# Issue-order edges and four dummy matmuls at the start of a transformer-block kernel

## Chip, cores, metric

The kernel runs on one core of a Trainium2 chip. The metric is the device time of one execution in microseconds (us); lower is better. The span that a profile shows, from the first to the last instruction, is about 1.8 us shorter than the device time of the same execution (739.5 against 741.27 us in the profile before).

Engines are named as in the profile: PE is TensorE's matmul, PEld its weight loads, DVE is VectorE, ACT is ScalarE, POOL is GpSimd, SP is SyncE.

## The reference

One block: layer norm, a projection to q, k and v, linear attention with 32 heads, an output projection with a residual, then layer norm, a gated feed-forward part and a second residual. Inputs are bf16; S = 2048 tokens, D = 1024, F = 3584.

```python
phi = lambda t: jnp.where(t > 0, t + 1, jnp.exp(t)) + 1e-6
q, k, v = split_heads(layernorm(x) @ wqkv)
kv  = einsum("bhsd,bhse->bhde", phi(k), v);  z = einsum("bhsd->bhd", phi(k))
h   = x + merge_heads((phi(q) @ kv) / (phi(q) . z + 1e-6)) @ wo
n   = layernorm(h)
out = h + (relu(n @ W_gate) * (n @ W_up)) @ W_down
```

## The kernel before

The change touches only the start of the kernel. There, tokens come in tiles of 128. A tile is normalised, transposed so that its features lie on the partitions, and multiplied with the K weights. The first four tiles are transposed on PE through one PSUM buffer, later ones by DMA. The first tile is normalised on VectorE, the others on ScalarE. Sixteen dummy matmuls on zeros run before the first data have come.

```python
    PE_T = 4          # tiles that PE transposes
    SPIN = 16         # dummy matmuls
    ...
        load_x(atiles[0])            # order of the loads
        load_w(wk_sb, 0, D)          # K weights, first column half
        load_x(atiles[1])
        load_w(wk_sb, 1, D)          # K weights, second column half
        load_x(atiles[2])
        load_x(atiles[3])
        for j in range(2):
            load_w(wv_sb, j, 2 * D)

        def ln_T(t):
            ...
            for k in range(2):       # VectorE: statistics of two halves, then their aggregate
                nc.vector.bn_stats(out=stats[:, k, :], in_=x_sb[:, k * NW:(k + 1) * NW])
            nc.vector.bn_aggr(out=mv[:], in_=stats[:])
            nc.scalar.activation(out=lnv, in_=mv[:, 1:2], func=ACT.Ln, bias=LN_EPS, scale=1.0)
            nc.scalar.activation(out=rstd, in_=lnv, func=ACT.Exp, scale=-0.5)
            if t == atiles[0]:
                ...                  # VectorE normalises tile 0 in two halves
                transpose_in(t, xn)
                return
            nc.vector.scalar_tensor_tensor(out=nmr, in0=mv[:, 0:1], scalar=-1.0, in1=rstd, op0=ALU.mult, op1=ALU.mult)
            nc.scalar.activation(out=xn[:], in_=x_sb[:], func=ACT.Identity, bias=nmr, scale=rstd)
            ...                      # later tiles: transposed by DMA
            transpose_in(t, xn)

        def transpose_in(t, xn):
            s, i, r = place(t)
            for k in range(2):       # one PSUM buffer ("D", bufs=1) for all halves
                pt = pspool.tile([P, KH, P], BF16, tag="D", bufs=1, name="tp")
                for kc in range(KH):
                    nc.tensor.transpose(pt[:, kc, :], xn[:, (k * KH + kc) * P:(k * KH + kc + 1) * P], ident[:])
                (nc.scalar.copy if k else nc.vector.tensor_copy)(
                    out=xT[s][i][:, k * KH:(k + 1) * KH, r:r + P], in_=pt[:])
    ...
        def k_plain(t):              # K of one tile: 8 matmuls for each column half
            ...
            for j in range(2):
                ps = pspool.tile([P, NW], FP32, tag="AE"[j], bufs=2, name="kp")
                for kc in range(KC):
                    nc.tensor.matmul(ps[:], lhsT=xT[s][i][:, kc, r:r + P], rhs=wk_sb[:, kc, js], ...)
                ...                  # exp on ScalarE, two VectorE instructions
    ...
        with tc.high_priority():
            ...
            for n in range(SPIN):
                nc.tensor.matmul(spin[:], lhsT=zero[:, 0:P], rhs=zero[:], start=True, stop=True)
            ln_T(atiles[0])
        ln_T(atiles[1])
        todo = atiles[2:8]
        for t in units[0]:
            k_plain(t)
            ln_T(todo.pop(0))
        new_v(0)
        for n, t in enumerate(units[0]):
            v_plain(t)
            ...
            if n == 1:
                sums_unit(1)
                k_sums()             # VectorE: sums of K weights, needed by the units after the first
```

The order in this text isn't the order on VectorE: the scheduler has brought the first of the four `k_sums` additions (L133 in the profile) forward, and it runs among the first tiles, at 10.77 us.

## Time and profile before

| What | Value | Where it is read |
|---|---|---|
| time, three executions | 740.27 us median (739.84 to 740.81) | the timed runs |
| time of the profiled execution | 741.27 us, mean clock 0.998 | the profile's own run |
| PE busy | 724.0 of 739.5 us (98%) | page, part 1 |
| longest PE wait after the dummies began, in the first 45 us | 2.1 us, for the copy of tile 0's first half | list of waits |
| granted clock, 9.58 to 13.14 us | 0.52 | table of stretches |

How to read PE busy: the records of pipelined matmuls overlap in it. K matmuls that start 0.22 us apart are listed with 0.38 us each. So it doesn't measure the distance from PE's peak. Here it serves only to find stretches in which PE has nothing to do, and for these it is good enough.

The timeline of PE in the kernel before, at its start. The columns are start, length, engine, line, operation, tiles, shapes, count, and in brackets the idle time before it and what ended it.

```profile
5.42 1.83 PE L400 MATMUL spin<-zero 128*128 128x512 bf16 x6
7.09 0.39 PE L299 MATMUL tp<-ident,xn 128*128 128x128 bf16 x4
9.58 0.58 PE L299 MATMUL tp<-ident,xn 128*128 128x128 bf16 x4 [2.10 <-DVE xT L300]
9.96 3.18 PE L347 MATMUL kp<-pq_mem,xT 128*128 128x512 bf16 x7
12.94 0.41 PE L299 MATMUL tp<-ident,xn 128*128 128x128 bf16 x4
13.20 0.38 PE L347 MATMUL kp<-pq_mem,xT 128*128 128x512 bf16 x1
```

Tile 0's first four transposes end at 7.48 us, the second four can't start before the buffer is copied out, and PE stands still for 2.1 us. Then seven K matmuls take 3.18 us, about 0.43 us from one start to the next, twice the 0.22 us of the warm ones later on. A column half of K needs one half of the weights.

The timeline of VectorE over the same time shows why the copy was late.

```profile
7.71 1.29 DVE L272 BATCH_NORM_STATS2 stats<-x_sb 128x6 f32<-128x512 bf16 x2 [1.24 <-DMA x_sb<-in_A_x_dram]
9.03 0.21 DVE L274 BATCH_NORM_AGGREGATE mv<-stats 128x2 f32<-128x12 f32 x1
9.16 0.37 DVE L300 COPY xT<-tp 128x512 bf16<-128x512 bf16 x1
...
10.77 1.23 DVE L133 TENSOR_TENSOR pq_mem<-pq_mem 128x2048 f16<-128x2048 bf16 x1 [0.87 <-DMA pq_mem<-in_A_wqkv_dram]
13.40 0.42 DVE L300 COPY xT<-tp 128x512 bf16<-128x512 bf16 x1 [1.40 <-PE tp L299]
```

The copy at 9.16 stands in VectorE's queue behind tile 1's statistics, although VectorE was idle for 1.24 us before these. L133 waits for the second half of the K weights, so its start, 10.77, marks when that half has landed.

The table of stretches of the kernel before. After the stretch and its length come the busy time of PE with the number of instructions, the same for PEld, DVE, ACT and POOL, then the granted clock, the DMA share and GB/s.

```profile
7.10:9.58 2.48, 0.38 (x6) 0.26 (x4) 1.78 (x4) 0.28 (x2) 0.00 (x0) 1.00 1.09 351
9.58:13.14 3.56, 3.56 (x15) 1.64 (x14) 1.38 (x2) 1.84 (x3) 0.00 (x0) 0.52 1.07 361
13.14:20.00 6.86, 6.66 (x42) 3.22 (x41) 6.60 (x17) 4.56 (x11) 0.00 (x0) 1.00 1.08 365
```

The clock of 0.52 in the second row is the half speed that the K matmuls showed.

### The profile page before, as it was taken

What the parts mean: (1) busy time and instruction counts of PE and PEld (TensorE: products, weight loads), DVE (VectorE), ACT (ScalarE), POOL (GpSimd) and SP (SyncE); (2) the same over time, 40 slices, a digit from 0 to 9 for tenths busy, and PEclk for the clock granted to TensorE, in tenths of its full rate; (3) what the DMA queues carried; (4) which work ended last, traced back from release to release, by engine and by line L of the source; (5) the groups of instructions that cost most, each with busy time, mean ns of one, the idle gap of its engine ahead of it and who ended that gap; (6) DMA issues with size and microseconds to landing.
All of it is one profiled execution on the core that took longest, in us unless ns stands there. A gap on an engine that the chain in (4) does not pass through costs nothing.

```text
span 739.5 us, 10552 instructions
## 1 busy us (share of the span) xinstructions
PE 724.0 (98%) x3967; PEld 382.7 (52%) x4020; DVE 563.7 (76%) x992; ACT 321.5 (43%) x580; POOL 5.6 (1%) x44
## 2 busy tenths in 40 slices
PE   8999999999999999999999999999999999999997
PEld 3444555444444444444444444444444458888566
DVE  5997644676798767778778777877786479996797
ACT  4877554778887644434344444444445120000000
POOL 0000000000000000000000000000000000000000
PEclk9999999999999999999999999999999999999999
DMA  9666002169987426164638359575583399987822
GB/s 315 153 145 170 1 1 67 48 149 218 237 168 181 124 73 206 43 193 134 198 117 242 110 177 283 171 219 194 170 277 121 129 398 339 331 288 299 295 76 82
DMA packets 146594, 132.02 MB, mean 179 GB/s; under 512 B 50928, under 2 KB 128112, under 8 KB 146544
## 3 DMA queue, kind: packets, MB, share of 16 engines
q1 hardware_dynamic: 135536, 123.30, 55.4%
q10 hardware_dynamic: 11008, 8.06, 3.4%
q8 instruction: 31, 0.51, 0.3%
q14 instruction: 19, 0.16, 0.1%
HBM read 79.95 MB, written 39.85 MB: 162 GB/s over the span
## 4 chain that ended last, share of the span: by engine, by line
PE 78%; DVE 8%; ACT 7%; DMA 5%; issue 1%; SPq 0%; DVEq 0%; POOL 0%; ACTq 0%
PE accA L821 22%; PE accY L821 8%; PE accX L821 8%; PE accA L1153 8%; PE Aq L314 3%; PE accA L982 3%; PE attn L557 3%; PE accX L1153 3%; PE Aq L454 3%; PE accY L1153 2%; DMA hn<-hn 2%; ACT hn L570 2%; PE Eq L314 2%; PE accY L982 2%; PE accX L982 2%
## 5 line engine op out<-in xcount | busy, mean ns | idle before, releaser
L831 ACT ACTIVATE gu<-gu 128x512 bf16<-128x512 bf16 x72 | 45.4, 631 | 131.4 <-DVE gu L830 131.4
L826 ACT COPY snap<-accA 128x1024 f32<-128x1024 f32 x72 | 72.5, 1008 | 36.4 <-PE accA L821 36.3
L821 PEld LDWEIGHTS <-tu 128*128 128x128 f16 x384 | 37.6, 98 | 45.3
L821 PEld LDWEIGHTS <-tg 128*128 128x128 f16 x384 | 37.6, 98 | 45.3
L557 PE MATMUL attn<-wo_mem,oT 128*128 128x512 bf16 x247 | 58.1, 379 | 2.3 <-DVE o_sb L534 1.0
L830 DVE TENSOR_TENSOR gu<-accY,snap 128x1024 bf16<-128x1024 f32 x36 | 43.9, 1220 | 10.0 <-ACT snap L826 10.0
L821 PE MATMUL accA<-hn,tu 128*128 128x512 f16 (+1 forms) x192 | 49.3, 379 | 0.0
L821 PE MATMUL accA<-hn,tg 128*128 128x512 f16 (+1 forms) x192 | 49.3, 379 | 0.0
L830 DVE TENSOR_TENSOR gu<-accX,snap 128x1024 bf16<-128x1024 f32 x36 | 43.9, 1219 | 6.3 <-PE accX L821 3.7
L154 ACT COPY u<-Aq 128x512 f32<-128x512 f32 x54 | 31.1, 580 | 36.2 <-PE Aq L314 19.3
L1153 PEld LDWEIGHTS <-x 128*128 128x128 f16 (+1 forms) x448 | 43.8, 98 | 5.5
L821 PEld LDWEIGHTS <-wg 128*128 128x128 bf16 x288 | 28.2, 98 | 34.0
L821 PEld LDWEIGHTS <-wu 128*128 128x128 bf16 x288 | 28.2, 98 | 34.0
L557 PEld LDWEIGHTS <-oT 128*128 128x128 bf16 x256 | 24.6, 97 | 32.2 <-issue 4.1
L834 DVE TENSOR_TENSOR hq<-gu 128x512 bf16<-128x512 bf16 x48 | 20.3, 423 | 14.3 <-ACT gu L831 14.2
L314 PEld LDWEIGHTS <-xT 128*128 128x128 bf16 (+1 forms) x192 | 18.6, 98 | 23.8 <-issue 2.4
L534 DVE TENSOR_TENSOR o_sb<-nd,rd 128x384 bf16<-128x384 f32 (+1 forms) x48 | 23.2, 509 | 8.6 <-ACT rd L533 6.6
L1153 PEld LDWEIGHTS <-xs 128*128 128x128 f16 x280 | 27.4, 98 | 3.2
L982 PEld LDWEIGHTS <-x 128*128 128x128 bf16 (+1 forms) x168 | 16.5, 98 | 19.6
L560 DVE SCALAR_TENSOR_TENSOR x_res<-attn,x_res 128x512 bf16<-128x512 f32 x32 | 22.0, 686 | 6.1 <-PE attn L557 5.9
L1159 DVE TENSOR_TENSOR snap<-accA,u 128x1024 f32<-128x1024 f32 x16 | 19.5, 1220 | 8.0 <-PE accA L1153 7.9
L821 PE MATMUL accA<-hn,wu 128*128 128x512 bf16 x96 | 24.6, 379 | 0.0
(234 smaller groups left out, 1406.1 us busy)
## 6 DMA issues: line engine op xcount, KB each, us to landing
x<-x_dram SPq DMA_DIRECT2D x17, 896.0 KB, 8.1
x_dram<-hq SPq DMA_DIRECT2D x28, 512.0 KB, 3.0
wg<-in_B_W_gate_dram SPq DMA_DIRECT2D x14, 512.0 KB, 5.1
wu<-in_B_W_up_dram SPq DMA_DIRECT2D x14, 512.0 KB, 7.3
wraw<-in_B_W_down_dram SPq DMA_DIRECT2D x14, 512.0 KB, 4.8
x_dram<-hq SPq DMA_DIRECT2D x28, 256.0 KB, 2.5
t_dram<-wt SPq DMA_DIRECT2D x28, 256.0 KB, 2.2
xd<-x_dram SPq DMA_DIRECT2D x6, 896.0 KB, 7.3
```

The source lines that it names most:

```text
L154: nc.scalar.copy(out=snaps[nm, v], in_=bank[v][:])
L314: nc.tensor.matmul(ps[:], lhsT=left[m - 1][:, kc, r + v * P:r + (v + 1) * P], rhs=right[m - 1][:, kc, :], start=(start and kc == 0), stop= ...
L454: nc.tensor.matmul(ps[:], lhsT=rq[m - 1][:, kc, (c + v) * P:(c + v + 1) * P], rhs=left[m - 1][:, kc, :], start=(start and kc == 0), stop=( ...
L534: nc.vector.tensor_tensor(out=ov[:, c0:c0 + n], in0=ndv[:, :, 0:P].rearrange("p k (h e) -> p k h e", h=HPC), in1=rd[:, 0:n, :].unsqueeze(3 ...
L557: nc.tensor.matmul(ps[:], lhsT=st["oT"][:, c, :], rhs=wo_sb[:, c, j * NW:(j + 1) * NW], start=(c == 0), stop=(c == KC - 1))
L560: nc.vector.scalar_tensor_tensor(out=h_sb[:, j * NW:(j + 1) * NW], in0=ps[:], scalar=1.0, in1=h_sb[:, j * NW:(j + 1) * NW], op0=ALU.mult, ...
L821: nc.tensor.matmul(ps[:, v, :], lhsT=w[v][n - 1][:, kc, :], rhs=left[n - 1][:, kc, :], start=(t is not None and kc == 0), stop=(kc == KH - ...
L826: nc.scalar.copy(out=st[nm][:], in_=halves(st["A"]))
L830: add(out=g[:], in0=halves(st[nm]), in1=st[base][:], op=ALU.add)
L831: nc.scalar.activation(out=g[:, 0, :], in_=g[:, 0, :], func=ACT.Relu)
L982: nc.tensor.matmul(ps[:, t * NW:(t + 1) * NW], lhsT=x_tile(n, s, kh)[:, f, (t0 + t) * P:(t0 + t + 1) * P], rhs=w_tile(n, kh)[:, f, :], sta ...
L1153: nc.tensor.matmul(pv[:, tt, :], lhsT=left(m)[:, f, tt * P:(tt + 1) * P], rhs=right(m)[:, f, :], start=(t is not None and f == 0 and tt % ...
```

## The change

The intent is to take the 2.1 us out. The copy is put ahead of tile 1's statistics, four dummies keep PE busy while it runs, and the K weight sums are kept behind tile 1's offset (`nmr`), so that they can't jump the queue in the new order. `issue_after` adds an edge of issue order on the same engine.

```diff
+        copied, offset = {}, {}
 ... in ln_T
-            nc.vector.scalar_tensor_tensor(out=nmr, ...)
+            offset[t] = nc.vector.scalar_tensor_tensor(out=nmr, ...)
 ... in transpose_in
                 pt = pspool.tile([P, KH, P], BF16, tag="D", bufs=1, name="tp")
+                if k == 1 and t == atiles[0]:
+                    with tc.issue_after(last.ins):
+                        spin_up(4)
                 for kc in range(KH):
-                    nc.tensor.transpose(...)
-                (nc.scalar.copy if k else nc.vector.tensor_copy)(
+                    last = nc.tensor.transpose(...)
+                copied[t, k] = (nc.scalar.copy if k else nc.vector.tensor_copy)(
 ... at the start
-            for n in range(SPIN):
-                nc.tensor.matmul(spin[:], ...)
+            def spin_up(n):
+                for _ in range(n):
+                    nc.tensor.matmul(spin[:], ...)
+            spin_up(SPIN)
             ln_T(atiles[0])
-        ln_T(atiles[1])
+        with tc.issue_after(copied[atiles[0], 0].ins):
+            ln_T(atiles[1])
 ... after the second V tile
-                k_sums()
+                with tc.issue_after(offset[atiles[1]].ins):
+                    k_sums()
```

More of the change, by code (lines that the diff above doesn't have):

```diff
@@ L286, in ln_T @@
                 return
-            nc.vector.scalar_tensor_tensor(out=nmr, in0=mv[:, 0:1], scalar=-1.0, in1=rstd, op0=ALU.mult, op1=ALU.mult)
+            offset[t] = nc.vector.scalar_tensor_tensor(out=nmr, in0=mv[:, 0:1], scalar=-1.0, in1=rstd,
+                                                       op0=ALU.mult, op1=ALU.mult)
             nc.scalar.activation(out=xn[:], in_=x_sb[:], func=ACT.Identity, bias=nmr, scale=rstd)
@@ L297, in transpose_in @@
                 pt = pspool.tile([P, KH, P], BF16, tag="D", bufs=1, name="tp")
+                if k == 1 and t == atiles[0]:
+                    with tc.issue_after(last.ins):
+                        spin_up(4)
                 for kc in range(KH):
-                    nc.tensor.transpose(pt[:, kc, :], xn[:, (k * KH + kc) * P:(k * KH + kc + 1) * P], ident[:])
-                (nc.scalar.copy if k else nc.vector.tensor_copy)(
+                    last = nc.tensor.transpose(pt[:, kc, :], xn[:, (k * KH + kc) * P:(k * KH + kc + 1) * P], ident[:])
+                copied[t, k] = (nc.scalar.copy if k else nc.vector.tensor_copy)(
                     out=xT[s][i][:, k * KH:(k + 1) * KH, r:r + P], in_=pt[:])
@@ L398, in block_kernel @@
             spin = pspool.tile([P, NW], FP32, tag="A", bufs=2, name="spin")
-            for n in range(SPIN):
-                nc.tensor.matmul(spin[:], lhsT=zero[:, 0:P], rhs=zero[:], start=True, stop=True)
+            def spin_up(n):
+                for _ in range(n):
+                    nc.tensor.matmul(spin[:], lhsT=zero[:, 0:P], rhs=zero[:], start=True, stop=True)
+            spin_up(SPIN)
             ln_T(atiles[0])
-        ln_T(atiles[1])
+        with tc.issue_after(copied[atiles[0], 0].ins):
+            ln_T(atiles[1])
         todo = atiles[2:8]
```

## The prediction

> **What bounds the kernel now.** The page of the profile has PE busy 98% of a 739.5 us span, so nearly all the time is dense matmul work that the change doesn't touch. Only the start can move. The stretch table gives PE 0.38 us of busy time between 7.10 and 9.58 us, and a granted clock near 0.5 between 9.5 and 13.0 us; after that PE is over 97% busy up to 41 us.
>
> The timeline shows how this comes about. The first tile's first four transposes end at 7.48 us. The copy of that half out of PSUM is queued on VectorE behind tile 1's statistics (two BATCH_NORM_STATS2 from 7.71 us, the aggregate at 9.03), so it runs at 9.16 to 9.53. The second half's transposes use the same PSUM buffer and start at 9.58: PE idles 2.1 us, the largest PE wait before 60 us in the list of waits. The second half's ScalarE copy then falls behind tile 1's normalisation and starts at 11.08.
>
> The weight loads of the last three dummies come 0.2 us apart instead of 0.43, so the clock had risen at about 6.3 us. [...] up at 6.3, down near 9.7, up again at 13.1. So the first K matmuls (9.96 to 13.14) run at 0.43 us apart instead of about 0.22.
>
> **What the change does.**
> - The copy (0.37 us) starts at about 7.55 instead of 9.16. Tile 1's statistics slip only some 0.2 us, as its x lands at 7.69.
> - Four dummies fill PE while the copy runs: 4 x 0.22 = 0.9 us warm, 1.7 us cold, to about 8.4 us. They may hold the second transposes back by 0.3 us[...].
> - Second transposes at about 8.4 instead of 9.58, ScalarE copy at about 8.8 instead of 11.08 (I expect it ahead of tile 1's normalisation), first K matmuls from about 8.6, warm, done by about 10.3 instead of 13.2.
> - The offset edge only forbids a new order: the first K weight sum (1.23 us) already followed tile 1's offset (9.74) and starts when the second weight half lands, at 10.77. It removes nothing.
>
> **How much is critical.** The second half of the K weights, landed at about 10.7, caps the gain: tile 0's second column half can start at about 10.8 instead of 13.2, 2.4 us earlier. Then VectorE limits: from 13.4 to 33 us it has almost no idle time, and tile 2's normalisation (ending 18.06) fed its transposes just in time (18.12). VectorE gains mainly its idle 12.0 to 13.4, about 1.4 us, so PE will give back up to 1 us waiting for tile 2. I expect 1.4 to 2.2 us to survive to the end, since PE is the limit later.
>
> **Predicted:** 738.5 us, 8 in 10 within 737.0 to 740.2. Faster by over 2%: 0.005; within 2%: 0.985; slower: 0.01.
>
> **What would show it.** Right: copy at about 7.6, granted clock 1.0 throughout 7 to 13 us, no PE wait of 2 us before the second transposes, the second K column half at about 10.8, first V matmul at about 25.5 instead of 27.3. Wrong in a step: clock still 0.5 after 9.7; second ScalarE copy still after tile 1's normalisation; a new PE wait for tile 2's normalisation near 16 us as large as the gain.
>
> **What would make it wrong.** A new instruction order later in the kernel; [...] VectorE or the transposing DMAs taking the whole gain back by 41 us.

The marked cuts took out a rule on what lowers and restores the clock, which no run of this case shows. 2.4 us at tile 0's second column half, less up to 1 us of new waiting for tile 2, gave 1.4 to 2.2 us, and their middle, 1.8 us, taken from the median of 740.27 us gives 738.5. That the first K matmuls would run warm, 0.22 us apart, rested on assumption.

## The result

| | before | after |
|---|---|---|
| median of the runs of the same rounds | 740.24 us (739.84 to 740.81, 6 runs) | 740.32 us (739.82 to 741.80, 6 runs) |
| ratio after / before | | 1.0003, 95% interval 0.9990 to 1.0016 |

The ratio is the mean time of one kernel's runs over that of the other's runs of the same rounds, so it isn't quite the ratio of the medians. The time didn't change. The forecast of 738.5 us, range 737.0 to 740.2, was wrong: the gain of 1.4 to 2.2 us didn't come.

And yet the profile after shows nearly every step that the prediction asked for. PE's timeline of the changed kernel:

```profile
6.52 0.39 PE L305 MATMUL tp<-ident,xn 128*128 128x128 bf16 x4
6.75 1.03 PE L408 MATMUL spin<-zero 128*128 128x512 bf16 x4
7.61 0.39 PE L305 MATMUL tp<-ident,xn 128*128 128x128 bf16 x4
7.83 1.89 PE L353 MATMUL kp<-pq_mem,xT 128*128 128x512 bf16 x8
10.71 1.02 PE L353 MATMUL kp<-pq_mem,xT 128*128 128x512 bf16 x4 [0.98 <-DMA pq_mem<-in_A_wqkv_dram]
```

The second transposes start at 7.61 instead of 9.58, the first eight K matmuls run 0.22 us apart, and tile 0's second column half starts at 10.71 instead of 11.66 (the prediction had taken 13.2 from the profile before). VectorE's timeline has the copy first:

```profile
6.95 0.42 DVE L306 COPY xT<-tp 128x512 bf16<-128x512 bf16 x1 [0.50 <-PE tp L305]
7.71 1.29 DVE L274 BATCH_NORM_STATS2 stats<-x_sb 128x6 f32<-128x512 bf16 x2 [0.33 <-DMA x_sb<-in_A_x_dram]
...
10.76 1.23 DVE L133 TENSOR_TENSOR pq_mem<-pq_mem 128x2048 f16<-128x2048 bf16 x1 [0.86 <-DMA pq_mem<-in_A_wqkv_dram]
11.90 1.28 DVE L274 BATCH_NORM_STATS2 stats<-x_sb 128x6 f32<-128x512 bf16 x2
13.10 0.41 DVE L306 COPY xT<-tp 128x512 bf16<-128x512 bf16 x1
```

Two of PE's waits in the first 45 us of the changed kernel (what PE waited for, us in total, times, longest); the others are for the first dummy (1.2 us) and 0.5 us near the end of that stretch:

```profile
PE tp L305 <- DVE xT L306: 1.1, 2, 0.7
PE kp L353 <- DMA pq_mem<-in_A_wqkv_dram: 1.0, 1, 1.0
```

And its table of stretches, columns as above:

```profile
7.10:9.58 2.48, 2.48 (x16) 1.13 (x14) 1.77 (x4) 0.87 (x3) 0.00 (x0) 1.00 1.09 353
9.58:13.14 3.56, 2.25 (x13) 1.00 (x12) 2.54 (x5) 2.13 (x4) 0.00 (x0) 1.00 1.07 362
```

The clock stays at 1.00. The 2.1 us gap is gone, and two waits have come in its place: 1.0 us for the K weights, which PE now reaches before they land, and 1.1 us for copies out of the one transpose buffer, the longest (0.7 us) for tile 1's, which now stands behind tile 2's statistics (11.90, then 13.10).

The first V matmul marks the end of the start. PE's timeline from 5 to 30 us has it in the profile before and then in the one after:

```profile
27.29 2.97 PE L365 MATMUL vp<-wv_sb,xT 128*128 128x512 bf16 x13
```

```profile
25.66 4.70 PE L371 MATMUL vp<-wv_sb,xT 128*128 128x512 bf16 x21
```

Between these two traces the changed kernel leads by 1.6 us there, and by 1.4 us still at 205 us. From there to 213 us the lead falls to 0.7, in a PE wait (the `attn` group for VectorE's `x_res`: 1.3 us against 0.7), and 0.7 is also the difference of the spans, 739.5 and 738.8. The obvious story is that a good start was half given back later. The experiments show that this story is wrong at its first step.

### The profile page after: what moved, and what is told of

It reads as the page before. It is cut to its first block, busy times and chain, and to the rows that moved or that the text cites. A ratio compares the mean times of both kernels' runs of the same rounds, so it can differ in the third digit from the quotient of the medians.

```text
span 738.8 us, 10561 instructions
## 1 busy us (share of the span) xinstructions
PE 722.4 (98%) x3971; PEld 382.3 (52%) x4024; DVE 563.8 (76%) x992; ACT 321.8 (44%) x580; POOL 5.6 (1%) x44
## 4 chain that ended last, share of the span: by engine, by line
PE 77%; DVE 9%; ACT 6%; DMA 5%; issue 2%; SPq 0%; DVEq 0%; POOL 0%; ACTq 0%
PE accA L833 22%; PE accX L833 8%; PE accY L833 8%; PE accA L1165 8%; PE Aq L320 3%; PE accA L994 3%; PE accX L1165 3%; PE attn L569 3%; PE Aq L466 3%; PE accY L1165 2%; ACT hn L582 2%; PE Eq L320 2%; DMA hn<-hn 2%; PE accY L994 2%; PE accX L994 2%
## 5 line engine op out<-in xcount | busy, mean ns | idle before, releaser
L833 PE MATMUL accA<-hs,tu 128*128 128x512 f16 x96 | 24.6, 379 | 0.0
```

Of the source, the lines that this page charges most:

```text
L833: nc.tensor.matmul(ps[:, v, :], lhsT=w[v][n - 1][:, kc, :], rhs=left[n - 1][:, kc, :], start=(t is not None and kc == 0), stop=(kc == KH - ...
```

## The experiments

Three explanations were open.

- **Clock by chance (P).** The half-clock stretch in the first profile of before was chance, and the typical execution of before doesn't have it. Then the 1.6 us were never there to be gained.
- **Weight landing (W).** The start is tied to the landing of the second half of the K weights; whatever PE does before, tile 2 follows that landing by a fixed interval. Then only a few tenths can be won.
- **Give-back (G).** The start gain is real, and later waits take it back.

All kernels computed correct results. "Before" beside a run means the runs of the unchanged kernel on the same chip in the same rounds.

### The same two kernels once more

The edit is none (a comment).

> The kernel before, unchanged, once more: noise floor, and a second sample of the clock. Theory P[...]: the half-clock window at 9.6 to 13.0 us in the first profile of before[...]; most runs of before do not have it. Then the mean clock in most runs is 0.999 to 1.000, those at about 0.997 to 0.998 are 1 to 1.7 us longer, and a profile without that window has its first V matmul at about 26.0 us or earlier instead of 27.3. Theory G (give-back): the start differs by 1.6 us from the changed kernel in every profile, and the lead is lost later, near 205 to 213 us; then first V matmul at about 27.3 again. Ratio 1.000 within 0.001 either way.

> The changed kernel once more. Both theories: ratio 0.999 to 1.001 to before. First V matmul at 25.6 to 25.8 us[...] if the dummies keep the clock up. G: the lead over before drops at the attention output (205 to 213 us) from 1.5 to 0.7 us or less. P: no drop there beyond 0.3 us when compared with a profile of before of full clock.

Times: before_again 740.43 us median (739.6 to 741.68), ratio 1.0000 (0.9986 to 1.0013); after_again 740.01 us (739.53 to 741.22), ratio 0.9996 (0.9983 to 1.0010). The profiled executions took 739.6 and 739.65 us. The first V matmul came at 25.59 us in before_again, as P expected, and at 25.19 us in after_again, earlier than the 25.6 to 25.8 expected, because the K weights landed 0.47 us earlier than in the first profile of after.

PE's timeline in the second profile of the *unchanged* kernel:

```profile
6.29 0.39 PE L299 MATMUL tp<-ident,xn 128*128 128x128 bf16 x4
9.15 0.38 PE L299 MATMUL tp<-ident,xn 128*128 128x128 bf16 x4 [2.47 <-DVE xT L300]
9.37 1.72 PE L347 MATMUL kp<-pq_mem,xT 128*128 128x512 bf16 x7
11.27 0.38 PE L299 MATMUL tp<-ident,xn 128*128 128x128 bf16 x4 [0.18 <-ACT xT L300]
25.59 4.70 PE L365 MATMUL vp<-wv_sb,xT 128*128 128x512 bf16 x21
```

And its stretches:

```profile
7.10:9.58 2.48, 0.43 (x5) 0.32 (x5) 1.94 (x5) 0.48 (x3) 0.00 (x0) 1.00 1.09 350
9.58:13.14 3.56, 3.38 (x22) 1.71 (x21) 2.67 (x4) 2.23 (x4) 0.00 (x0) 1.00 1.08 362
```

The gap is still there, and even longer (2.5 us), with the copy just as late behind tile 1's statistics. But the seven K matmuls take 1.72 us instead of 3.18, because the clock stayed at 1.00. The span is 737.8 us, shorter than that of the changed kernel's first profile. And the fifth K matmul, the first that needs the second half of the weights, starts at 10.28 us, 0.04 us after that half has landed (10.24). The cap that the prediction named for the changed kernel was already reached by the unchanged one.

VectorE's copy for tile 1, which stood at 13.40 in the half-clock profile, behind tile 1's late transposes:

```profile
11.69 0.42 DVE L300 COPY xT<-tp 128x512 bf16<-128x512 bf16 x1
```

Why did the clock fall in one execution and not in the other? No run shows a rule for it, but the traces show this. In the first profile the weight loads of the dummies come 0.43 us apart until about 6.2 us and 0.2 us apart after it; the trace's clock record begins at 6.16 us with 1.00, is half from 9.57 to 12.98 us, and then 1.00 again: two stretches of 3.41 us. "Window" stands for such a stretch in what follows. The window from 6.16 to 9.57 us held the whole gap; PE streamed in only 33% of it (my estimate, from the starts and the spacing of matmuls and transposes; whether the clock counts a transpose like a matmul isn't shown), and the next one ran at half clock. In the second profile, reckoned in the same steps from where its dummies come 0.22 us apart, a window's edge fell inside the gap: the two windows that share it were 57% and 53% busy (the same estimate), and the clock stayed at 1.00. That a window with little work is followed by one at half clock is my reading of these two profiles, and it is the clock theory below. It isn't shown as a rule: a window at 38% in a later profile (copy_kedge3, the same estimate) was not followed by half clock.

With the landing of the K weights (L133) as zero, the starts of all profiles can be compared. The landing itself moves by 0.8 us from run to run among kernels with the same load order. The table is worked out from the starts of single instructions in the traces; L133 is the time at which its queue came to it, some 0.06 us ahead of the starts in the timelines. Two kernels that move other things (b_s24, ck_ks2) are left to the text.

| profile | L133 (us) | tile 2's normalisation starts, after L133 | first V matmul, after L133 |
|---|---|---|---|
| before, first profile (half clock) | 10.71 | 6.12 | 16.58 |
| before with SPIN=10 (half clock) | 11.02 | 6.61 | 17.08 |
| before, second profile | 10.27 | 4.85 | 15.32 |
| before with three dummies | 10.20 | 4.83 | 15.30 |
| after, first profile | 10.69 | 4.58 | 14.96 |
| after, second and third profile | 10.22, 10.40 | 4.58 | 14.96, 14.97 |
| after with a longer q product (a_q3, below) | 10.20 | 4.58 | 14.96 |
| after without the four dummies, three profiles | 10.18 to 10.35 | 4.58 | 14.96 to 14.97 |
| the same with tile 1 loaded earlier | 11.85 | 4.58 | 14.96 |

So the 1.62 us between the first profiles (16.58 − 14.96) have two parts: 16.58 − 15.32 = 1.26 us are the clock of that one execution of before, and 15.32 − 14.96 = 0.36 us are the change. The profile's chain of work shows why so little is left. In before_again it runs from tile 1's x (landed at 7.25) through tile 1's normalisation (9.50), ScalarE's copy of tile 0's second half (10.65) and tile 1's transposes (11.27) to tile 1's copy (11.69) and tile 2's statistics. In the first profile of after it runs from the K weights (landed at 10.67) through L133 (10.76) to tile 2's statistics (11.90). The change replaces one chain by another that is hardly shorter.

The two profiles of before speak against give-back too. At the first V matmul the second leads by 1.70 us (27.29 against 25.59), and its span is still shorter by 1.7 us (739.5 against 737.8). The three ScalarE lines that carry this, tile 2's normalisation in the first and second profiles of before and in the first of after:

```profile
16.82 1.24 ACT L288 ACTIVATE xn<-x_sb,sma 128x1024 bf16<-128x1024 bf16 x1 [0.55 <-ACT e L349]
```

```profile
15.12 1.24 ACT L288 ACTIVATE xn<-x_sb,sma 128x1024 bf16<-128x1024 bf16 x1 [0.54 <-ACT e L349]
```

```profile
15.27 1.24 ACT L291 ACTIVATE xn<-x_sb,sma 128x1024 bf16<-128x1024 bf16 x1 [0.37 <-DVE sma L289]
```

Compared by the clock on the wall, the unchanged kernel is even the earlier one here (15.12 against 15.27), because its weights landed 0.43 us earlier (VectorE's L133 starts at 10.33 against 10.76).

### The parts of the change alone

copy_kedge is the changed kernel without its dummies, both edges kept:

```diff
-                if k == 1 and t == atiles[0]:
-                    with tc.issue_after(last.ins):
-                        spin_up(4)
```

> The changed kernel without its four dummies; orders of VectorE and ScalarE as in the changed kernel. If the dummies matter for the clock: half clock for about 3.4 us somewhere between 6 and 14 us and first V matmul 0.5 to 1.7 us later than 25.7. If only the earlier copy matters: first V matmul at 25.3 to 25.8. Total: within 0.1% of the changed kernel in both cases if the start is given back later (G); up to 1.5 us longer under P.

dum_3 is dummies without order; it has three because then the order of VectorE's instructions is that of before:

```diff
-                        spin_up(4)
+                        spin_up(3)
-        with tc.issue_after(copied[atiles[0], 0].ins):
-            ln_T(atiles[1])
+        ln_T(atiles[1])
```

> The kernel before with three dummies after the first four transposes (0.65 us warm), copy still behind the statistics; orders of VectorE and ScalarE as before. Tests the clock alone: if three dummies suffice[...], granted clock 1.0 from 9.6 to 13 and first V matmul 1.0 to 1.7 us earlier than 27.3; if not, as before. Total: under P equal to a full-clock run of before, 740.0 +- 0.4 us.

Times: copy_kedge 739.29 us (738.98 to 742.21), ratio 0.9991 (0.9976 to 1.0007); dum_3 740.20 us (739.25 to 741.94), ratio 0.9998 (0.9984 to 1.0012). Neither differs from before by more than chance.

PE's timeline of dum_3 shows what dummies alone do:

```profile
6.35 0.81 PE L408 MATMUL spin<-zero 128*128 128x512 bf16 x3
9.07 0.38 PE L305 MATMUL tp<-ident,xn 128*128 128x128 bf16 x4 [1.91 <-DVE xT L306]
```

They fill 0.8 us at the front of the gap and leave 1.9 us of it, and the second transposes start at 9.07, much as in before_again (9.15). After the landing, everything is as in the second profile of before (4.83 and 15.30 in the table). The first V matmul came at 25.50 us, 1.8 us ahead of 27.29, but this isn't the dummies' doing: before_again has 25.59 without them. As before_again kept its clock too (1.00 from 7.10 to 13.14 us in both), dum_3 doesn't show whether three dummies protect it.

PE's timeline of copy_kedge:

```profile
7.09 0.39 PE L302 MATMUL tp<-ident,xn 128*128 128x128 bf16 x4
7.99 0.38 PE L302 MATMUL tp<-ident,xn 128*128 128x128 bf16 x4 [0.52 <-DVE xT L303]
8.21 1.89 PE L350 MATMUL kp<-pq_mem,xT 128*128 128x512 bf16 x8
10.31 1.24 PE L350 MATMUL kp<-pq_mem,xT 128*128 128x512 bf16 x5 [0.21 <-DMA pq_mem<-in_A_wqkv_dram]
```

The edges alone shorten the gap to 0.5 us. PE still waits for the weights at 10.31, so the four dummies of the full change fill time that PE spends waiting anyhow. Without them the windows at the start were at least 62% busy (the same estimate) and the granted clock was 1.00 from 7.10 to 20.00 us, so in this run the clock didn't need them. The first V matmul came at 25.26 us. One order isn't as expected: ScalarE takes tile 2's logarithm (13.46) ahead of the copy (13.58), which stands first in after.

### Moving the number of dummies

If the clock theory holds, half clock at the start should return when PE has more idle time there. In before, SPIN is set to 10 and to 24.

```diff
-    SPIN = 16
+    SPIN = 10        # b_s10;  b_s24 has 24
```

> The kernel before with 10 warm-up dummies instead of 16 (they end near 5.4 us; orders of the other engines as before). Clock theory (P): [...] the first K matmuls run 0.43 us apart in this profile, first V matmul near 27.3 us as in the first profile of before, and the median is 1 to 2 us longer than before (ratio 1.0015 to 1.0025). Rival (VectorE chain alone decides the start, clock or no clock): first V matmul at 25.6 +- 0.3 and ratio 1.000 +- 0.0008.

> The kernel before with 24 warm-up dummies (orders of the other engines as before; the copy still behind the statistics). They hold the first transposes back to about 8.3 us, which costs nothing as the copy only comes at 9.1, and leave PE idle about 0.5 us instead of 2.5. P: no half-clock window near 9.6[...], first V matmul at 25.5 to 25.8, and times like the full-clock runs of before, 740.2 +- 0.4 median, without the runs at 742 and over. Rival: same first V matmul, but runs over 742 still occur, so those are not the start's clock.

b_s10 took 742.21 us (741.61 to 742.77), ratio 1.0024 (1.0011 to 1.0037). PE's timeline:

```profile
5.98 0.40 PE L299 MATMUL tp<-ident,xn 128*128 128x128 bf16 x4 [1.02 <-DVE xn L283]
9.89 0.58 PE L299 MATMUL tp<-ident,xn 128*128 128x128 bf16 x4 [3.51 <-DVE xT L300]
10.27 3.19 PE L347 MATMUL kp<-pq_mem,xT 128*128 128x512 bf16 x7
```

The gap is 3.5 us, seven K matmuls take 3.19 us again, and half clock lasts from 7.54 to 14.37 us, two windows (6.83 us), after windows that were 25% and 31% busy (the same estimate). One window was expected; with two, the first V matmul came at 28.10 us instead of 27.3. All five runs had a mean clock of 0.995 to 0.997 (the profiled one 0.995). So with more idle time the start ran at half clock in the one execution that shows it, the other four have a mean clock to match, and the kernel took some 2 us more. This supports the clock theory, with one profile.

b_s24 took 742.38 us (740.07 to 743.54), ratio 1.0024 (1.0008 to 1.0041), and missed its expectation. In its profile (740.56 us) PE was at full speed from 6.99 us on (by the spacing of the dummies: 16 from 4.57 us on take 4.82 us), but 24 dummies delayed tile 0's transposes to 9.22 us (8.3 expected), and the first V matmul to 26.25 us (25.5 to 25.8 expected), 16.01 after L133. Two of the other five runs were at clock 1.0 and 0.999 (740.07 and 741.5 us); three were at 0.997 to 0.998 and took 743.25 to 743.54 us. So runs at 743 us occur that by the clock theory the longer row of dummies should have prevented, as the rival in the expectation had it. Whether they lost their clock at the start or later isn't known, and as the dummies also delay the start, this kernel is no clean test.

The mean clock tells how often this happens. A profile with one half-clock window has 0.998 (before) or 0.997 (a_q3, below), one with two has 0.995 (b_s10), and those without have 0.999 or 1.000 (one window of 3.41 us at half clock takes 0.0023 off a mean over 740 us). By this measure, of the 40 timed runs of before whose clock is on record, from three chips, 35 had no such window and took 740.17 us on average (standard deviation 0.56); five had one and took 742.3. Of the changed kernel's 17 runs, 16 had none and took 740.18 us; one took 741.8. At equal clock the two kernels are equal to 0.01 us, with an uncertainty of some 0.3 us. Where in the kernel those five runs lost their clock isn't known, because only profiled executions show it.

### Does a start gain reach the end?

The give-back theory is tested from the other side. a_q3 is the changed kernel with its first q product computed three times: eight extra matmuls, 1.7 us, at about 122 us, with all orders kept. If later waits have slack, the end moves by less than 1.7 us.

```diff
         def mm(ps, m, v, start):
-            for kc in range(KH):
-                nc.tensor.matmul(ps[:], ...)
+            for _ in range(3 if (s, c, m, v) == (0, 0, 1, 0) else 1):
+                for kc in range(KH):
+                    nc.tensor.matmul(ps[:], ...)
```

> The changed kernel with eight more matmuls (about 1.7 us of PE) in the first q product, near 100 us; all orders kept. If PE carries a delay to the end, 1.5 to 1.9 us longer than the changed kernel (ratio 1.0020 to 1.0026 to before), so that a gain at the start would have reached the end too. If there is slack behind it (G: the waits near 160 and 212 us are for transfers that do not move), less than 0.9 us longer (ratio under 1.0012).

a_q3 took 745.02 us (743.28 to 745.52), ratio 1.0060 (1.0047 to 1.0072), 4.4 us more than before, where 1.5 to 1.9 more than the changed kernel were expected. Against after_again, matmul by matmul, its delay is about 1.8 us from 144 to 262 us, 3.0 at 264 and 4.7 at 270; then 4.0 from 274 to 549 and 5.4 from 609 us to the end. The step up to 270 is a fall of the clock, which the stretches of a_q3 show:

```profile
264.33:267.75 3.42, 1.32 (x7) 0.61 (x7) 1.57 (x5) 3.05 (x8) 0.00 (x0) 1.00 0.20 77
267.75:271.18 3.43, 3.43 (x10) 1.24 (x9) 1.12 (x2) 1.77 (x3) 0.00 (x0) 0.50 0.13 27
```

PE was busy for 1.32 of 3.42 us (39%), and in the next 3.43 us the granted clock was 0.50. The low share stands where the feed-forward part begins and PE waits for ScalarE. In a_q3's list of waits and then in after_again's:

```profile
PE Aq L740 <- ACT m L154: 2.5, 1, 2.5
```

```profile
PE Aq L739 <- ACT m L154: 1.3, 1, 1.3
```

So a delay is passed on in full, and here it grew. Why the wait grew by 1.2 us, and what came after 549 us, isn't known; the fall of the clock isn't needed for a large delay, as the one run at clock 1.0 took 743.28 us, 3.1 more than the changed kernel at full clock, and one at 0.999 took 745.52. A delay is also not an advance: the run shows no slack after 122 us that swallows 1.6 us, but not that a lead would survive. That is shown better by the two profiles of before, where 1.7 us of lead reach the end. Together they leave give-back little room as the explanation of a vanished 1.6 us. They don't exclude that the last 0.3 us of an early start are lost. In the pair of full-clock profiles whose weights landed at nearly the same time, after_again leads before_again by 0.2 to 0.5 us until 262 us and by nothing after 263, where its wait of 1.3 us stands against 1.0. That is one pair, so it isn't shown as a rule.

The 1.3 us wait at 205 to 213 us in the first profile of after comes and goes. after_again, the same code, doesn't have it (0.7 us, as in before_again), but after_3 has it (1.3), and so has b_s10 (1.3), which lacks the change. So it isn't tied to the change, but what brings it isn't known.

### Is the landing of the K weights the anchor?

Two edits of copy_kedge. ck_swap loads tile 1 ahead of the K weights:

```diff
         load_x(atiles[0])
-        load_w(wk_sb, 0, D)
         load_x(atiles[1])
+        load_w(wk_sb, 0, D)
         load_w(wk_sb, 1, D)
```

> The changed kernel without dummies, with tile 1's x loaded ahead of the first K weight half (orders of PE, VectorE and ScalarE kept). Theory W (from the landing of the second K weight half on, VectorE's in-order work is the chain; it starts with the first K weight sum): tile 2's normalisation starts 4.6 +- 0.1 us after that sum and the first V matmul 15.0 +- 0.1 us after it, as in all five profiles with the early copy, although tile 1's statistics can start over 2 us earlier. Rival X (the chain runs through tile 1's x): both come 0.5 us or more earlier against the sum. Time: W 739.3 to 740.2, ratio 0.9990 to 1.0003; X under 0.9985.

ck_ks2 puts the K weight sums behind tile 2's offset, so that the 1.2 us of L133 no longer stand ahead of tile 2's statistics:

```diff
-                with tc.issue_after(offset[atiles[1]].ins):
+                with tc.issue_after(offset[atiles[2]].ins):
                     k_sums()
```

> The changed kernel without dummies, with the K weight sums held behind tile 2's offset instead of tile 1's (later orders shift too). W: without the 1.2 us sum in front, tile 2's normalisation starts 3.3 to 4.2 us after the landing of the second K weight half instead of 4.6; PE, which has 24 matmuls (5.2 us) and transposes to do from the landing, is then the limit, so the first V matmul comes at most 0.5 us earlier (14.5 to 14.9 after the landing). Total within 0.1% either way: VectorE has the sum still to do later. Rival X: 4.6 and 15.0 stay.

ck_swap took 742.44 us (741.78 to 743.84), ratio 1.0031 (1.0017 to 1.0044). The expected time was missed: the second half of the K weights landed 1.6 us later, which I hadn't foreseen. VectorE's timeline:

```profile
11.91 1.23 DVE L133 TENSOR_TENSOR pq_mem<-pq_mem 128x2048 f16<-128x2048 bf16 x1 [1.75 <-DMA pq_mem<-in_A_wqkv_dram]
```

But as a test of the anchor it is the best run. Everything came 1.6 us later, with exactly the same intervals after the landing (4.58 and 14.96 us), and at full clock the kernel was some 2 us slower. The landing sets the start of the changed kernel. One thing isn't separated: tile 2's x lands 0.68 us after that half (10.67 and 11.35 in the first profile of after, 11.82 and 12.50 here), so ck_swap moves both landings together.

ck_ks2 took 739.87 us (739.75 to 742.74), ratio 1.0000 (0.9985 to 1.0015). Tile 2's normalisation still starts some 4.6 us after the landing (10.23 us by PE's first matmul with that half, then 14.84), although L133 has left that place; 3.3 to 4.2 us were expected. VectorE, and then ScalarE's normalisation of tile 2:

```profile
10.87 1.88 DVE L274 BATCH_NORM_STATS2 stats<-x_sb 128x6 f32<-128x512 bf16 x3 [0.72 <-DMA x_sb<-in_A_x_dram]
12.67 0.41 DVE L303 COPY xT<-tp 128x512 bf16<-128x512 bf16 x1
...
15.40 1.21 DVE L133 TENSOR_TENSOR pq_mem<-pq_mem 128x2048 f16<-128x2048 bf16 x1
```

```profile
14.84 1.24 ACT L291 ACTIVATE xn<-x_sb,sma 128x1024 bf16<-128x1024 bf16 x1 [0.61 <-DVE sma L289]
```

The statistics now had to wait for tile 2's x (the 0.72 us of idle time before them), the scheduler put a third statistics half in the free place, and tile 1's copy came behind it at 12.67, no earlier than in copy_kedge (12.70). My sub-claim, that the 1.2 us of the sum are a link of the chain that can be taken out, therefore isn't borne out: take them away, and tile 2's x and another order fill the time. The first V matmul came some 0.25 us sooner after the landing, within the 14.5 to 14.9 expected, and the time didn't show it.

### Is the version without dummies better?

copy_kedge had the lowest median, so it ran twice more, once beside the changed kernel (after_3). The edits are none.

> The changed kernel without its four dummies, again: was its 0.9991 real? If it is a gain at full clock, median 739.3 +- 0.4 and ratio 0.9985 to 0.9995; if chance, median 740.0 +- 0.3 and ratio 0.9995 to 1.0005.

> The changed kernel without its four dummies, a third time. If it really beats the changed kernel, full-clock runs at 739.0 to 739.7 and 0.3 us or more below those of the changed kernel in this call; if its two earlier results were chance, within 0.3 us of it. First V matmul 14.96 us after the landing, so that a gain over the changed kernel could not come from the start.

> The changed kernel a third time, beside the next run. If the change is worth what the profiles of full clock show at the first V matmul (0.35 us, 0.05%), ratio 0.9990 to 1.0003, which the noise (0.5 us from run to run) does not tell from 1. First V matmul 14.96 us after the landing of the second K weight half, again.

The results: copy_kedge2 739.79 us (738.99 to 741.18), ratio 0.9996 (0.9984 to 1.0008); copy_kedge3 740.00 us (738.91 to 740.90), ratio 0.9993 (0.9979 to 1.0007); after_3 740.02 us (739.59 to 740.90), ratio 0.9996 (0.9982 to 1.0010). Over all its 17 runs, copy_kedge's 16 runs at full clock average 739.76 us, against 740.17 for before and 740.18 for after. That would be 0.4 us, or 0.05%. By the expectations, both repeats fit chance: copy_kedge2 with 739.79 us and 0.9996, and copy_kedge3 just so, as its full-clock runs average 739.93 us, 0.29 below after_3's 740.22. Pooled over the rounds, the lead over before is 0.41 us with a 95% uncertainty of 0.38, for a kernel that was picked for its first result. Each of the three intervals contains 1, so I don't call it shown; the edges without the dummies are at least no worse than the change as a whole.

## Why the prediction was wrong

The step that failed is the baseline. The prediction said: "So the first K matmuls (9.96 to 13.14) run at 0.43 us apart instead of about 0.22", and took this one profiled execution for the kernel. From it followed "2.4 us earlier" for tile 0's second column half, VectorE's "idle 12.0 to 13.4, about 1.4 us", and "I expect 1.4 to 2.2 us to survive". The runs show that the half clock belonged to that execution. The "2.4 us" were a misreading besides: 13.2 wasn't the start of that column half, which began at 11.66 even at half clock, and at full clock it begins at 10.28, 0.04 us after its weights land, without the change. From the point that was to give 2.4 us, nothing was left to gain. At full clock the unchanged kernel reaches its first V matmul 15.3 us after the landing of the K weights, and the changed one 15.0: the change is worth 0.36 us there, not 1.6. In its second profile, before's tile-1 copy on VectorE starts at 11.69 us and not 13.40, so the idle time that VectorE was to gain isn't there.

The warning was on the page. The profiled execution took 741.27 us with a mean clock of 0.998, and the three timed runs lay between 739.84 and 740.81. The profile was of a run 1.0 us slower than the median, and I forecast a gain of 1.8 us from it against that median. The prediction even listed a clock that falls elsewhere among its risks, but only for the changed kernel, not for the kernel before.

Point by point:

- Right: the copy early (7.6 predicted, 6.95 measured), clock 1.0 from 7 to 13 us, no 2 us wait before the second transposes, ScalarE's second copy ahead of tile 1's normalisation (8.03 instead of 11.08 us), tile 0's second column half at 10.7 (10.8 predicted), the first V matmul at 25.66 (25.5 predicted). These describe the changed kernel; the gain was to be the distance from the kernel before.
- Right: the landing of the second half of the K weights caps the start. ck_swap showed how rigid that cap is. Overlooked: the unchanged kernel at full clock starts that column half at the same cap.
- Wrong in kind: "PE will give back up to 1 us waiting for tile 2". PE's new waits are 1.0 us for the K weights and 1.1 us for copies out of the transpose buffer, 0.7 of it for tile 1; none is for tile 2's normalisation. They aren't a loss: in the second profile of before the same time is one gap of 2.5 us.
- Wrong: 25.5 "instead of 27.3". At full clock before has 25.59 (second profile), with weights that landed 0.4 us earlier.
- The offset edge "removes nothing": nothing in the runs contradicts this. It was never taken out by itself, so it isn't shown either.
- The dummies were to keep the clock up. With them it was 1.00 from 7.10 to 13.14 us, but copy_kedge without them kept the clock in three profiles too (mean clocks 0.999, 1.000 and 1.000). No run shows a gain from them.

What could remain as a gain is small. Before had 5 of 40 runs with a half-clock window, the changed kernel 1 of 17. Five of 40 at 2.1 us each (742.3 − 740.17) are 0.27 us on average, so even without a single such window the mean would fall by no more than that. The means over all runs, 740.44 and 740.28 us, differ by 0.16 us, well inside the scatter.

Open are: why a 1.3 us wait near 212 us comes and goes; in which part of the kernel the low-clock timed runs lost their clock, and so how often before starts at half clock (one of its two profiles did); whether the 0.36 us of the start are lost near 263 us; what lowers the clock (windows at 25 to 39% busy, by my estimates, were followed by half clock, and one at 38% was not); and whether copy_kedge's 0.4 us are real.

## What to carry to other kernels

Before a step is costed from a trace, compare the profiled execution's time and mean clock with the timed runs; if it is slower by about the gain that you hope for, profile the kernel a second time. When two traces are compared, set zero at the last load that the stage waits for, because a landing that moves by half a microsecond hides or feigns such gains. Here a PE gap of 2.5 us ahead of a load that landed late cost at most 0.36 us at full clock; 1.26 us more went in the execution in which the K matmuls after the gap (2.1 us there) ran at half clock. And before a start is called late, look at what the instructions before it wait for: the K matmul at 13.20, which I took for the first that uses the second half of the weights, was the eighth, and the fifth already used it.
